# Two slots of expert 0 taken out of the routed order: found, gathered and begun inside attention

## The chip, the cores and the metric

One core of a Trainium2 chip runs the whole program in one launch. The time is device microseconds of that core; the number compared is the median over runs, and one further execution was recorded by the hardware profiler. The engines are TensorE (PE in the profile, its weight loads PEld), VectorE (DVE), ScalarE (ACT), GpSimd (POOL) and SyncE (SP, which issues most DMAs).

## The reference

Three stages follow one another. Attention runs over keys and values that are averaged over blocks of 8 positions; a mixture of 8 experts takes the best expert for each of 4,608 tokens; a dense layer of width 2,048 with a squared ReLU ends it.

```python
k_p = k.reshape(B, H, Sp, pool, D).mean(axis=3)            # 8 batches, 8 heads, 576 -> 72, D = 64
attn = softmax(scale * q @ k_p^T);  x = attn @ v_p         # x: 4608 x 512
e_idx = np.argmax(x @ w_gate, axis=1)
for e in range(E):                                         # 8 experts, 512 -> 1024 -> 512
    h = np.maximum(x[mask] @ w1[e], 0.0);  ye = h @ w2[e]
    out[mask] = gate_w[mask, None] * eom[mask, e, None] * ye
h = x @ w_in                                               # 512 -> 2048
g = s * np.maximum(h, 0) ** 2 + b;  return g @ w_out       # 2048 -> 512
```

All is in float32. Large products are taken as three products of split operands (high x high, high x low, low x high), so one product of a 128-token tile with a 512 x 1024 matrix is 24 matmuls of 128x512.

## The kernel before

**Attention** (`attention`) goes through 36 tiles of 128 tokens in one software pipeline: in turn `t` the steps `s1` to `s5` work on tiles `t+1`, `t`, `t-2`, `t-3` and `t-4`. `s5` divides by the sum of the exponentials (`rec`), writes the gate logits `lg` and the output tile `x` (L362), and SP stores `x` to DRAM (`xd`, L365). Keys and values land in four raw buffers (`krs`, `vrs`), one of them lent by the raw room of the experts' second weights. `hooks` run at the end of given turns; they load and split expert 0's first weights (`wa`).

**Routing** (`Router`) takes the tiles in six batches (8, 8, 8, 6, 4, 2 tiles). `steps` finds each token's expert (`oh`), counts with small matmuls into the PSUM tile `pr` (L565 to L579), and ranks. DVE steps of it are put singly between those of attention by `fill`. After the last batch `finish` turns ranks into slot numbers, compares them with the slot index (`ro_eq`, L676), and inverts the permutation by 40 matmuls into `inv` (L684), once for the first three slots and once for the rest; `kp_idx` (L690) is then the list of tokens of every slot, and `tables` (L717 to L740) writes which slots change expert (`kp_chg`, `kp_nxt`). Between these steps stand matmuls on the identity whose result nobody reads (`warm`, L77).

**Experts** (`experts`). The tokens of one expert fill whole slots of 128, so there are at most 43 slots; the table `total` says how many are used. For slot `i`: `gather(i)` on POOL fetches its 128 tokens (`xg`, L1009), `tr(i)` transposes them on PE (`pt`, L1018) and splits them on ACT and DVE (`xh`, `xl`, L804/L805), `l1(i)` is the first layer (24 matmuls, L1028 to L1030, into `bank`), `trh` transposes the hidden layer (`th`, L1042), `cut_h` splits it (`hh`, `hl`), and `l2` is the second layer (24 matmuls, `py`, L1058). `l2` of slot `i-1` stands between `l1(i)` and `trh` of slot `i`.

`sw1(i)` and `sw2(i)` (`switch`) are conditional: where slot `i` begins a new expert, ACT and DVE split its weights and SP loads the ones after; in any case ACT, DVE and SP read the flag `kp_chg` and branch (L855, L856). The matmuls of `l1(i)` wait for the semaphores that ACT and DVE reach behind this branch.

Into the slots `side(i, part)` puts work for later stages: a step of `Doubles` (`db.step`), which turns float64 weights of the dense stage into pairs of float32 on ACT, DVE and POOL (`dt`, `wo`; L929 to L946), and once, at slot 0, `close_ranks` (L749 to L780 on DVE), which makes the final positions and the slots' start rows.

**Order.** The program is issued as written, on five in-order engines; nothing reorders it. Buffers and waits follow from pools of tiles.

Of the kernel before, what the change touches and what calls it, by code (L numbers as in the profile page):

```python
# [49 lines left out]
def attention(ctx, tc, c, q, k, v, wg, wog, xd, lg, ro, spare, hooks):  # L50
# [21 lines left out]

    def warm(n):

        w = ps.tile([P, 512], F32, tag="pf", name="warm")
        for _ in range(n):
            nc.tensor.matmul(w[:, 0:P], lhsT=ident, rhs=ident, start=True, stop=True)  # L77
# [265 lines left out]
    def s5(t, pv):  # L343
# [16 lines left out]
        def rest():  # L360
            x = p3.tile([P, 2, 4, D], F32, tag="x", name="x", bufs=5)
# [156 lines left out]
class Router:  # L518


    def __init__(self, ctx, tc, c, lg, kp):
# [120 lines left out]
    def finish(self, psv, inv):  # L642
        nc, V, p1, kp, c = self.nc, self.nc.vector, self.p1, self.kp, self.c
# [1 line left out]
        til = p1.tile([P, E], I32, name="ro_til")
# [1 line left out]
        toff = p1.tile([P, E], F32, name="ro_toff")
        ot = p1.tile([P, E, NT], F32, name="ro_ot")
        sf = p1.tile([P, NT], F32, name="ro_sf")
# [999 lines left out]
```

## Time and profile before

| | |
|---|---|
| median of 3 runs | 1447.56 us (1447.36 to 1448.45) |
| profiled execution | 1446.02 us, span 1444.1 us |
| PE busy | 1412.4 us, 98% of the span |
| DVE, ACT, POOL busy | 828.1, 709.4, 429.3 us |
| attention and routing, to the first matmul of a slot | 0 to 200.5 us |
| experts (39 slots) | 200.5 to some 690 us |
| dense stage | to 1444 us |

The page gives the busy time of each engine, 40 slices of the span, the chain that ended last, and the costliest groups of instructions. Where PE is busy without a gap the time is the sum of its work; where it waits, the trace names the engine and line that released it. The number of slots used is the second layer's count, 624 high-half matmuls at 16 a slot: 39. The reference's own routing, with its tokens put in the order of the kernel's tiles, gives the experts 1018, 55, 333, 239, 827, 724, 24 and 1388 tokens: 8, 1, 3, 2, 7, 6, 1 and 11 slots; of the first 2,048 tokens in that order 863 go to expert 0.

### The profile page before, as it was taken

To read this page: it belongs to the slowest core of one execution; us is meant where nothing else is said; L and a number is where in the kernel's file an instruction comes from. 1 tells how busy PE (TensorE), PEld (TensorE's weight loads), DVE (VectorE), ACT (ScalarE), POOL (GpSimd) and SP (SyncE) were. 2 spreads that over 40 slices of the span, in tenths; PEclk is the share of its full clock that TensorE was granted. 3 is DMA by queue.
4 is the path that set the end of the run, shared out by engine and by line. 5 is a ranking of instruction groups with operands and counts; after the bars stand their busy time and mean duration, and the time that the engine had idled before them with its cause. 6 is when DMAs were issued, how large, how long until landed. Compare 5 with 4: busy or idle time off the path is not lost.

```text
span 1444.1 us, 23042 instructions
## 1 busy us (share of the span) xinstructions
PE 1412.4 (98%) x7612; PEld 1243.0 (86%) x7612; DVE 828.1 (57%) x1669; ACT 709.4 (49%) x1318; POOL 429.3 (30%) x579
## 2 busy tenths in 40 slices
PE   6999999999999999999999999999999999999998
PEld 5898978888888888887888988888888888889887
DVE  6788885487746567324666534634554463455333
ACT  3666623365534355223556555545555554555443
POOL 4998233444655558325320100000010000001001
PEclk9999999999999999999999999999999999999999
DMA  9995343277865768485665654465465446545441
GB/s 248 282 316 172 125 168 127 88 234 225 234 199 184 215 192 254 144 64 153 220 163 131 181 145 127 121 189 139 117 182 147 121 129 182 138 117 162 121 115 62
DMA packets 203040, 239.43 MB, mean 166 GB/s; under 512 B 66702, under 2 KB 114062, under 8 KB 202894
## 3 DMA queue, kind: packets, MB, share of 16 engines
q1 hardware_dynamic: 195502, 217.22, 54.2%
q0 software_dynamic: 7392, 20.49, 4.7%
q8 instruction: 63, 1.03, 0.3%
q14 instruction: 83, 0.68, 0.2%
HBM read 184.39 MB, written 43.83 MB: 158 GB/s over the span
## 4 chain that ended last, share of the span: by engine, by line
PE 44%; issue 8%; DVE 0%; ACT 0%; POOL 0%; DMA 0%; POOLq 0%; DVEq 0%; ACTq 0%
PE po L1439 8%; PE po L1438 8%; PE po L1437 7%; PE bank L1378 7%; PE bank L1379 7%; PE bank L1380 7%; PE py L1058 0%; POOL out L1449 0%; DMA ring<-ws 0%; DVE yo L1446 0%; POOLq L1645 0%; DVE y L1393 0%; ACT wb L1402 0%; DVE wb L1404 0%; ACT xg L1384 0%
## 5 line engine op out<-in xcount | busy, mean ns | idle before, releaser
L1401 ACT ACTIVATE r<-r,s_b 128x384 f32<-128x384 f32 x188 | 133.3, 709 | 275.4 <-DVE r L1394 247.8
L1449 POOL DMA_INDIRECT out<-yo,kp_pos x36 | 35.7, 991 | 662.9 <-ACT yo L1448 537.2
L1439 PE MATMUL po<-wo,wb 128*128 128x512 f32 x576 | 228.6, 397 | 0.0
L1438 PE MATMUL po<-wo,wb 128*128 128x512 f32 x576 | 227.6, 395 | 0.0
L1437 PE MATMUL po<-wo,wb 128*128 128x512 f32 x576 | 224.0, 389 | 0.0
L1058 PE MATMUL py<-wb,hh 128*128 128x512 f32 x624 | 191.2, 389 | 0.3 <-ACT hh L804 0.3
L1393 DVE TENSOR_TENSOR r<-bank,held 128x384 f32<-128x384 f32 x141 | 78.4, 556 | 183.1 <-PE bank L1380 181.1
L1378 PE MATMUL bank<-wa,ring 128*128 128x384 f32 x480 | 162.3, 338 | 1.0 <-ACT xg L1384 0.9
L1379 PE MATMUL bank<-wa,ring 128*128 128x384 f32 x480 | 162.1, 338 | 0.0
L1380 PE MATMUL bank<-wa,ring 128*128 128x384 f32 x480 | 161.0, 335 | 0.0
L1404 DVE TENSOR_TENSOR wb<-r,wb 128x384 fp32r<-128x384 f32 x188 | 105.3, 560 | 67.8 <-ACT wb L1402 67.4
L1058 PEld LDWEIGHTS py<-wb,hh 128*128 128x128 f32 x624 | 117.0, 188 | 24.7 <-ACT hh L804 0.5
L804 ACT ACTIVATE hh<-th 128x512 fp32r<-128x512 f32 x78 | 42.5, 595 | 180.1 <-PE th L1042 179.0
L1439 PEld LDWEIGHTS po<-wo,wb 128*128 128x128 f32 x576 | 107.9, 187 | 23.1
L1028 PE MATMUL bank<-wa,xh 128*128 128x512 f32 x312 | 125.5, 402 | 0.0
L931 POOL TENSOR_SCALAR dt<-dt 128x256 f32<-128x256 f32 x64 | 71.9, 1123 | 175.3 <-DVE dt L930 148.9
L1030 PE MATMUL bank<-wa,xl 128*128 128x512 f32 x312 | 122.1, 391 | 0.0
L1029 PE MATMUL bank<-wa,xh 128*128 128x512 f32 x312 | 121.6, 390 | 0.2 <-DVEq L856 0.2
L1058 PE MATMUL py<-wb,hl 128*128 128x512 f32 x312 | 120.5, 390 | 0.0
L1437 PEld LDWEIGHTS po<-wo,wb 128*128 128x128 f32 x576 | 108.2, 188 | 11.5
L1438 PEld LDWEIGHTS po<-wo,wb 128*128 128x128 f32 x576 | 107.9, 187 | 11.5
L1378 PEld LDWEIGHTS bank<-wa,ring 128*128 128x128 f32 x480 | 90.1, 188 | 16.2 <-ACT r L1390 4.6
(262 smaller groups left out, 2846.5 us busy)
## 6 DMA issues: line engine op xcount, KB each, us to landing
ring<-ws SPq DMA_DIRECT2D x336, 256.0 KB
wr<-in_moe_w SPq DMA_DIRECT2D x72, 512.0 KB
ws<-wf SPq DMA_DIRECT2D x16, 896.0 KB
ys<-y SPq DMA_DIRECT2D x37, 256.0 KB
xd<-x SPq DMA_DIRECT2D x36, 256.0 KB
q<-in_q SPq DMA_DIRECT2D x16, 512.0 KB
vr<-in_v SPq DMA_DIRECT2D x8, 1024.0 KB
dx<-in_moe_w_out SPq DMA_DIRECT2D x32, 256.0 KB
```

What stands on the lines that cost most here:

```text
L1028: nc.tensor.matmul(ph, lhsT=xh[:, k], rhs=wh[:, k, s], start=k == 0, stop=False)
L1029: nc.tensor.matmul(ph, lhsT=xh[:, k], rhs=wl[:, k, s], start=False, stop=False)
L1030: nc.tensor.matmul(ph, lhsT=xl[:, k], rhs=wh[:, k, s], start=False, stop=k == 3)
L1058: nc.tensor.matmul(py, lhsT=a, rhs=w, start=j == 0, stop=j == len(steps) - 1)
L1378: nc.tensor.matmul(o, lhsT=w[:, 0, k], rhs=xh[:, k], start=f, stop=False, skip_group_check=True)
L1379: nc.tensor.matmul(o, lhsT=w[:, 0, k], rhs=xl[:, k], start=False, stop=False, skip_group_check=True)
L1380: nc.tensor.matmul(o, lhsT=w[:, 1, k], rhs=xh[:, k], start=False, stop=False, skip_group_check=True)
L1401: lambda: nc.scalar.activation(out=r, in_=r, func=AF.Identity, scale=s_b[:, 0:1], bias=s_b[:, 1:2]),
L1404: [lambda: nc.vector.tensor_tensor(out=gl, in0=r, in1=gh.bitcast(F32), op=ALU.subtract)],
L1437: nc.tensor.matmul(o, lhsT=gh[:, s], rhs=wh, start=first, stop=False)
L1438: nc.tensor.matmul(o, lhsT=gh[:, s], rhs=wl, start=False, stop=False)
L1439: nc.tensor.matmul(o, lhsT=gl[:, s], rhs=wh, start=False, stop=last)
```

## The change

The first two slots are taken out of the sorted order. They hold the first 256 tokens of expert 0 among the first sixteen tiles (2,048 tokens; where there are fewer, `hole` empty places are counted to expert 0). `Router.ahead`, behind the second batch, finds them: 12 short DVE steps put between those of attention, one count and 20 inverting matmuls. `First` holds their work: two gathers on POOL at turn 28; eight transposes at turn `NT+2`, ahead of the last `s4`; the first layers of both slots (48 matmuls, `ph`), in pieces of 12, 8, 4, 8, 4 and 12 where the `warm` matmuls stood; the first slot's hidden layer transposed (`th`) and split. Expert 0's second weights are loaded and split in attention too (ACT and POOL, eight pieces each); POOL, not DVE, takes the low halves. `experts` begins with the second layer of slot 0, then the four `side` parts of slots 0 and 1, `tr(2)`, `tr(3)`, the hidden layer of slot 1, `sw1(2)`, and then the loop from slot 2.

`Router`'s tables and two buffers move into `wf`, a room kept from the start; the raw key and value buffers move into the room of the second weights; `x` has four buffers where it had five. `NSLOT` is 45 in place of 43. Line numbers of the changed kernel are its own: L541 is `First`'s first layer, L864 the inversion, L995 the low half of a split, L1058/L1059 the switch, L1228 `tr`, L1238 to L1240 `l1`, L1252 `trh`, L1268 `l2`, L1140 to L1156 `db.step`.

```diff
-    krs = [
-        one.tile([KB, NBLK, POOL * D], F32, name="kr"),
-        spare[0:KB, 0:NBLK * POOL * D].rearrange("p (j f) -> p j f", j=NBLK),
-    ]
-    vrs = [one.tile([P, NBLK, POOL * D], F32, name=f"vr{i}") for i in range(2)]
+    kv = NBLK * POOL * D
+    spare = wt.pool.tile([P, 8192], F32, tag="wb", name="kvr")
+    krs = [t[0:KB, 0:kv].rearrange("p (j f) -> p j f", j=NBLK) for t in (spare, wt.raw[1][0])]
+    vrs = [spare[:, kv * i:kv * i + kv].rearrange("p (j f) -> p j f", j=NBLK) for i in (1, 2)]
+    xbuf = [one.tile([P, DM], F32, name=f"x{i}") for i in range(3)] + [room]
+    xbuf = [t.rearrange("p (a h d) -> p a h d", a=2, h=4) for t in xbuf]
...
+        if t == 28:
+            first.gather(xd)
+        if t == NT + 2:
+            first.open()
+            first.turn(0, ps.tile([P, 512], F32, tag="pe", name="pt0"))
+            first.turn(1, ps.tile([P, 512], F32, tag="pf", name="pt1"))
...
-    warm(WARM[0])
+        if t == NT + 2:
+            first.cut(0)
     left, last = todo[:-5], todo[-5:]
     for f in last:
         f()
         if left:
             left.pop(0)()
+    first.layer(0, ps.tile([P, 2, 512], F32, tag="pv", name="ph0"))
+    first.run(12)
+    first.relu(0)
+    first.run(8)
     psv = later.pop()()
-    warm(WARM[1])
+    first.run(4)
     rest()
+    first.cut(1)
     for f in left:
         f()
+    def between():
+        first.relu(1)
+        first.layer(1, ps.tile([P, 2, 512], F32, tag="sc", name="ph1"))
+        first.run(8)
+        first.turn_h(ps.tile([P, 2, 512], F32, tag="pv", name="th0"))
+        first.run(4)
+        first.relu(0)
+    def behind():
+        first.high_h()
+        first.run(12)
+        first.relu(1)
     inv = [ps.tile([P, NSLOT], F32, tag=n, name="inv") for n in ("pq", "pe")]
-    ro.finish(psv, inv)
-    warm(WARM[2])
+    ro.finish(psv, inv, between, behind, first.low_h)
+    return first
...
+    def gather(self, xd):
+        t = self.parts(0, F32)
+        self.x = t[0:2]
+        self.hs = [t[2:4], t[0:2]]
+        for i in range(PRE):
+            self.nc.gpsimd.indirect_dma_start(
+                out=self.x[i], out_offset=None, in_=xd[0:SEEN * P, :],
+                in_offset=bass.IndirectOffsetOnAxis(ap=self.idx[:, i:i + 1], axis=0),
+            )
+    def turn(self, i, pt):
+        self.pt[i] = pt
+        for k in range(4):
+            self.nc.tensor.transpose(
+                out=pt[:, k * P:k * P + P], in_=self.x[i][:, k * P:k * P + P], identity=self.ident
+            )
+    def cut(self, i):
+        split(self.nc, *self.xs[i], self.pt.pop(i))
...
+    def layer(self, i, ph):
+        self.i, self.ph = i, ph
+        xh, xl = [x.rearrange("p (k n) -> p k n", n=P) for x in self.xs[i]]
+        wh, wl = [w.rearrange("p (k f) -> p k f", f=FE) for w in self.wt.a]
+        for n in range(2):
+            s = slice(n * 512, n * 512 + 512)
+            o = ph[:, n]
+            for k in range(4):
+                for x, w in ((xh, wh), (xh, wl), (xl, wh)):
+                    self.todo.append(
+                        lambda o=o, a=x[:, k], b=w[:, k, s], u=k == 0 and x is xh and w is wh, v=k == 3 and x is xl:
+                        self.nc.tensor.matmul(o, lhsT=a, rhs=b, start=u, stop=v)
+                    )
+    def run(self, n):
+        for _ in range(n):
+            self.todo.pop(0)()
+    def relu(self, n):
+        self.nc.scalar.activation(out=self.hs[self.i][n], in_=self.ph[:, n], func=AF.Relu)
+    def turn_h(self, th):
+        self.th = th
+        for n in range(2):
+            for k in range(4):
+                self.nc.tensor.transpose(
+                    out=th[:, n, k * P:k * P + P], in_=self.hs[0][n][:, k * P:k * P + P], identity=self.ident
+                )
+    def high_h(self):
+        for n in range(2):
+            self.nc.scalar.activation(out=self.hh[n], in_=self.th[:, n], func=AF.Copy)
+    def low_h(self):
+        for n in range(2):
+            self.nc.vector.tensor_tensor(
+                out=self.hl[n], in0=self.th[:, n], in1=self.hh[n].bitcast(F32), op=ALU.subtract
+            )
...
+PRE = 2
+SEEN = 16
+HOLE = PRE * P
+NSLOT = NT + E - 1 + PRE
+ROOM = 5120
 WIDE = 4
-SOON = 3
-WARM = (11, 12, 11)
+SOON = 5
...
+    def ahead(self, carry, alloc, later):
+        nc, V, c, kp, oh = self.nc, self.nc.vector, self.c, self.kp, self.kp["oh"]
+        hole, sf, ps = kp["hole"], self.tile([P, SEEN], F32), []
+        more = [self.tile([P, 1], F32) for _ in range(2)]
+        def settled():
+            while later:
+                later.pop()()
+            return ps[0]
+        def count():
+            ps[:] = [alloc()]
+            nc.tensor.matmul(ps[0][:, 0:E], lhsT=c["ones"], rhs=carry, start=True, stop=True)
+        def invert():
+            ps[:] = [alloc()]
+            order = [NT + t for t in range(WIDE)] + list(range(SEEN))
+            for i in order:
+                nc.tensor.matmul(
+                    ps[0][:, 0:PRE], lhsT=self.rv[:, i, :], rhs=self.eq[:, i % NT, 0:PRE],
+                    start=i == order[0], stop=i == order[-1],
+                )
+        sh = [P, SEEN, PRE]
+        return [
+            lambda: later.append(count),
+            lambda: V.tensor_scalar(
+                out=sf, in0=oh[:, 0, 0:SEEN], scalar1=-64.0, scalar2=64.0, op0=ALU.mult, op1=ALU.add
+            ),
+            lambda: V.tensor_tensor(out=sf, in0=sf, in1=self.ki[:, 0:SEEN], op=ALU.add),
+            lambda: V.tensor_scalar(
+                out=hole, in0=settled()[:, 0:1], scalar1=-1.0, scalar2=float(HOLE), op0=ALU.mult, op1=ALU.add
+            ),
+            lambda: V.tensor_tensor(
+                out=self.eq[:, 0:SEEN, 0:PRE], in0=c["iota_s"][:, 0:PRE].unsqueeze(1).to_broadcast(sh),
+                in1=sf.unsqueeze(2).to_broadcast(sh), op=ALU.is_equal,
+            ),
+            lambda: later.append(invert),
...
+            lambda: V.tensor_scalar(
+                out=kp["idx"][:, 0:PRE], in0=settled()[:, 0:PRE], scalar1=float(MID), scalar2=float(SEEN * P - 1),
+                op0=ALU.add, op1=ALU.min,
+            ),
+            lambda: V.tensor_tensor(out=more[1], in0=more[1], in1=hole, op=ALU.is_lt),
+            lambda: V.tensor_tensor(out=more[0], in0=more[0], in1=more[1], op=ALU.add),
+            lambda: V.tensor_tensor(out=self.sum[:, 0:1], in0=self.sum[:, 0:1], in1=more[0], op=ALU.add),
+            lambda: V.tensor_copy(out=carry[:, 0:1], in_=self.sum[:, 0:1]),
+        ]
...
-        compare(0, NT, 0, SOON)
+        compare(0, NT, PRE, SOON)
         for step in rows:
             step()
-        invert(inv[0], 0, SOON)
+        between()
+        invert(inv[0], PRE, SOON)
         for t in range(0, 24, 8):
             compare(t, t + 8, SOON, NSLOT)
-        index(inv[0], 0, SOON)
+        index(inv[0], PRE, SOON)
+        behind()
         compare(24, 32, SOON, NSLOT)
         compare(32, NT, SOON, NSLOT)
         invert(inv[1], SOON, NSLOT)
+        last()
         index(inv[1], SOON, NSLOT)
         self.tables()
...
+    c1 = wk[:, E + E * NT + NT:2 * E + E * NT + NT]
+    V.tensor_copy(out=c1, in_=cnt)
+    V.tensor_tensor(out=c1[:, 0:1], in0=c1[:, 0:1], in1=hole, op=ALU.subtract)
+    V.tensor_tensor_scan(out=c0, data0=c["one8"], data1=c1, initial=0.0, op0=ALU.mult, op1=ALU.add)
+    V.tensor_tensor(out=c0, in0=c0, in1=c1, op=ALU.subtract)
+    V.tensor_scalar(out=cs, in0=kp["oh"][:, 0], scalar1=hole, scalar2=None, op0=ALU.mult)
+    V.tensor_tensor(out=kp["pos"][:, SEEN:], in0=kp["pos"][:, SEEN:], in1=cs[:, SEEN:], op=ALU.subtract)
...
-    gather(0)
-    gather(1)
-    tr(0)()
     gather(2)
-    sw1(0)
-    tr(1)()
     gather(3)
-    wt.split(1)
-    sw2(0)
+    py = l2(room_y(), True, start.hh, start.hl)
+    second(1)
+    side(0, 0)
+    side(0, 1)
+    tr(2)()
+    gather(4)
+    th = trh(start.hs[1])
+    wt.raw_new(0)
+    second(0)
+    later = [tr(3)]
+    gather(5)
+    cut_h(th)
+    later.append(lambda: result(0, py))
+    side(1, 0)
+    side(1, 1)
+    sw1(2)
...
-    for i in range(NT - 1):
+    for i in range(PRE, NT - 1):
...
+        hooks.setdefault(25 + j, []).append(lambda j=j: wt.load(1, slice(0, 1), part=j))
+            hooks.setdefault(29 + j + what, []).append(lambda j=j, w=what: wt.piece(1, j, 8, w, nc.gpsimd))
```

On PE, in the routing of the last batch, the order before is this (`pr` is the last count, `tri`, `ones` and `oh` its operands, `inv` the inverted permutation):

```order
L574 MATMUL pr<-rcarry,ones 128x16
L579 LDWEIGHTS ones
L579 MATMUL pr<-oh,ones 128x8
L77 MATMUL warm<-ident 128x128 x12
L684 LDWEIGHTS rv
L684 MATMUL inv<-ro_eq,rv 128x3
```

And in the changed kernel, from the same count to the first inverting matmul (`ph_2631` and `ph_2688` are the first layers of slots 0 and 1, `th` the hidden layer of slot 0, `wf` the room that now holds the routing tables):

```order
L705 MATMUL pr<-oh,ones 128x8
L541 MATMUL ph_2631<-wa_114,first_2574 128x512 x2
L541 MATMUL ph_2631<-wa_115,first_2574 128x512
...
L541 MATMUL ph_2688<-wa_115,first_2574 128x512
L555 MATMUL th_2697<-ident,first_2066 128x128 x8
...
L541 MATMUL ph_2688<-wa_114,first_2574 128x512
L864 LDWEIGHTS wf
L864 MATMUL inv<-wf 128x3
```

Sixteen matmuls and eight transposes stand between the count and the inversion, where there were twelve `warm` matmuls.

On DVE, behind the last index, the order before has the split of slot 0's tokens (`xl`) and the switch next to the tables (`kp_nxt`, `kp_pos`); `close_ranks` (L749 and on) comes after it:

```order
L740 TENSOR_SCALAR kp_nxt<-ro_nx 1x44
L707 SCALAR_TENSOR_TENSOR kp_pos<-ki,rf 128x36
L805 TENSOR_TENSOR xl_2882<-pt,xh_2880 128x512
L855 TENSOR_LOAD kp_chg
L856 COMPARE_AND_BRANCH
```

In the changed kernel the switch that the first layer of slot 2 waits for stands behind `close_ranks` (L934 to L970, from which one row is shown), the split of slot 2's tokens and of slot 1's hidden layer (`hl`), and the four steps of `Doubles` (numbers behind a name tell buffers apart):

```order
L890 SCALAR_TENSOR_TENSOR kp_pos_92<-wf_116 128x36
...
L970 TENSOR_REDUCE kp_st_97<-dy_2919 1x1
L1140 TENSOR_SCALAR dt_2946<-dx_2841 128x256
...
L995 TENSOR_TENSOR xl0_2870<-pt_2959,xh0_2868 128x512
L995 TENSOR_TENSOR hl0_2876<-th_2967,hh0_2874 128x512
...
L1147 TENSOR_SCALAR dt_3005<-dt_3005 128x256
L1151 SCALAR_TENSOR_TENSOR dt_3005<-dx_2845,dt_3005 128x256
L995 TENSOR_TENSOR wo0_1_2840<-dt_2952,wo0_0_2839 128x256
L1058 TENSOR_LOAD kp_chg_95
L1059 COMPARE_AND_BRANCH
```

Thirty-nine DVE instructions stand between the tables and the first switch of the changed kernel, where there was one.

On PE, the changed kernel goes from the inversion straight to the second layer of slot 0 (`py`), and what follows is the first layer of slot 2, whose first matmul waits for ACT and whose second for DVE:

```order
L1268 MATMUL py_2880<-wb_2166,first01_2574 128x512 x23
L1228 MATMUL pt_2959<-ident_64,xg0_2866 128x128 [waits DMASW2_49]
L1228 MATMUL pt_2959<-ident_64,xg0_2866 128x128 x3
L1252 MATMUL th_2967<-ident_64,first00_2066 128x128 x4
L1252 MATMUL th_2972<-ident_64,first00_2066 128x128 x4
L1228 MATMUL pt_2993<-ident_64,xg1_2867 128x128 [waits DMASW3_49]
L1228 MATMUL pt_2993<-ident_64,xg1_2867 128x128 x3
L1059 UNCONDITIONAL_BRANCH
L1238 MATMUL bank0_2852<-wa0_114,xh0_2868 128x512 [waits Activation_49]
L1239 MATMUL bank0_2852<-wa1_115,xh0_2868 128x512 [waits DVE_49]
L1240 MATMUL bank0_2852<-wa0_114,xl0_2870 128x512
```

Before, the inversion was followed by `warm`, two `tr` and the first layer of slot 0.

## Rows read from the trace of the kernel before

**Rows 1.** Stretches: us, then busy us and count per engine, PEclk, DMA share.
```profile
144.00:180.00 36.00, 35.03 (x308) 33.03 (x307) 31.11 (x97) 22.33 (x60) 8.39 (x11) 1.00 0.40 127
...
187.00:201.00 14.00, 11.40 (x159) 10.39 (x157) 12.14 (x51) 0.97 (x3) 5.59 (x6) 1.00 0.43 133
```
**Rows 2.** Groups by line: busy us, mean ns, idle before.
```profile
L362 DVE TENSOR_TENSOR x<-pv,rec 128x512 f32<-128x512 f32 x36 | 24.5, 680 | 0.0
L77 PE MATMUL warm<-ident 128*128 128x128 f32 x68 | 8.3, 279 | 0.0
```
**Rows 3.** Timeline of PE, routing: start us, us, instruction, [idle before <-releaser].
```profile
186.13 0.19 PE L572 MATMUL pr<-oh,tri 128*128 128x32 bf16 x1
...
189.60 0.20 PE L569 MATMUL pr<-oh,ones 128*128 128x8 bf16 x2 [0.63 <-DVE oh L556]
...
192.77 2.31 PE L684 MATMUL inv<-ro_eq,rv 128*128 128x3 f16 x80
...
198.84 0.63 PE L1018 MATMUL pt<-ident,xg 128*128 128x128 f32 x4 [1.21 <-DVE ro_le L734]
...
200.51 0.47 PE L1028 MATMUL bank<-wa,xh 128*128 128x512 f32 x1
201.21 0.50 PE L1029 MATMUL bank<-wa,xh 128*128 128x512 f32 x1 [0.23 <-DVEq L856]
```
**Rows 4.** Timeline of PE, second layer of slot 0 to first layer of slot 2.
```profile
214.31 0.62 PE L1058 MATMUL py<-wb,hh 128*128 128x512 f32 x2
...
219.76 1.03 PE L1042 MATMUL th<-ident,hs 128*128 128x128 f32 x8
220.63 0.60 PE L1018 MATMUL pt<-ident,xg 128*128 128x128 f32 x4
220.98 0.48 PE L1028 MATMUL bank<-wa,xh 128*128 128x512 f32 x1
```
**Rows 5.** Timeline of DVE, from the last ranks to the first steps of Doubles.
```profile
186.46 0.19 DVE L619 TENSOR_TENSOR rmine<-pr,oh 128x32 f32<-128x32 f32 x1 [0.61 <-PE pr L579]
...
190.12 0.17 DVE L652 TENSOR_SCALAR ro_til<-pr 128x8 int32<-128x8 f32 x1
...
194.00 0.15 DVE L690 TENSOR_SCALAR kp_idx<-inv 128x3 int32<-128x3 f32 x1
...
195.12 0.20 DVE L690 TENSOR_SCALAR kp_idx<-inv 128x40 int32<-128x40 f32 x1 [0.34 <-issue]
...
199.03 0.18 DVE L707 SCALAR_TENSOR_TENSOR kp_pos<-ki,rf 128x36 int32<-128x36 int32 x1
200.24 0.69 DVE L805 TENSOR_TENSOR xl<-pt,xh 128x512 fp32r<-128x512 f32 x1 [1.03 <-ACT xh L804]
...
207.98 0.17 DVE L749 TENSOR_TENSOR_SCAN dy<-one,kp_cnt 128x8 f32<-128x8 f32 x1
...
213.17 0.27 DVE L930 TENSOR_SCALAR dt<-dx 128x256 int32<-128x256 int32 x1
213.37 1.27 DVE L805 TENSOR_TENSOR hl<-th,hh 128x512 fp32r<-128x512 f32 x2
```
**Rows 6.** Timeline of POOL, a gather and one step of Doubles.
```profile
195.06 1.20 POOL L1009 DMA_INDIRECT xg<-xd,kp_idx  x1 [1.91 <-DMA dx<-in_moe_w_out]
...
216.00 1.08 POOL L931 TENSOR_SCALAR dt<-dt 128x256 f32<-128x256 f32 x1
217.04 0.85 POOL L946 TENSOR_TENSOR dt<-dt,dx 128x256 int32<-128x256 int32 x1
```
**Rows 7.** A stretch near the start, as rows 1.
```profile
31.20:34.60 3.40, 3.40 (x15) 3.17 (x14) 2.89 (x9) 0.58 (x1) 0.00 (x0) 0.50 1.08 226
```
**Rows 8.** Timeline of PE around that stretch.
```profile
30.73 0.28 PE L168 MATMUL prl<-ident,kp 72*128 72x72 f32 x1 [1.92 <-ACT kbd L163]
...
31.37 2.13 PE L278 MATMUL sc<-kbd,qT 128*128 128x144 f32 x8
...
36.79 1.15 PE L278 MATMUL sc<-kbd,qT 128*128 128x144 f32 x8
```

More of the change, by code (lines that the diff above doesn't have):

```diff
@@ L71, in attention @@
     vps = [one.tile([P, NBLK + 1, D], F32, name=f"vp{i}") for i in range(2)]
[L73 to L77, printed above, removed]
     def load_kv(b, src, dst, n, j0=0, j1=NBLK):
@@ L360, in rest @@
         def rest():
[L361 removed]
+            x = xbuf[t % 4]
             nc.vector.tensor_tensor(
@@ L426, in attention @@
     later = []
+    first = First(nc, ident, wt, ro.kp["idx"])
     for t in range(NT + 4):
@@ new lines, in behind, with __init__, parts, open @@
+    def behind():
+        first.high_h()
+        first.run(12)
+        first.relu(1)
+    inv = [ps.tile([P, NSLOT], F32, tag=n, name="inv") for n in ("pq", "pe")]
+    ro.finish(psv, inv, between, behind, first.low_h)
+    return first
+class First:
+    def __init__(self, nc, ident, wt, idx):
+        self.nc, self.ident, self.wt, self.idx = nc, ident, wt, idx
+        self.pt, self.todo = {}, []
+    def parts(self, i, dt):
+        t = self.wt.raw_tile(0, i, dt, "first")
+        return [t[:, DM * j:DM * j + DM] for j in range(4)]
+    def open(self):
+        t = self.parts(1, F32R)
+        self.xs = [t[0:2], t[2:4]]
+        self.hh, self.hl = self.xs
+    def gather(self, xd):
[48 more added lines that the diff above has]
+            )
@@ L609, in steps @@
                 out += self.row(t)
-        return out
+        if b == SEEN:
+            out += self.ahead(carry, alloc, later)
+        return out
+    def ahead(self, carry, alloc, later):
[32 more added lines that the diff above has]
+            lambda: later.append(invert),
+            lambda: V.tensor_scalar(out=hole, in0=hole, scalar1=0.0, scalar2=None, op0=ALU.max),
+            lambda: V.tensor_tensor(out=more[0], in0=c["pvec"], in1=hole, op=ALU.is_lt),
+            lambda: V.tensor_scalar(out=more[1], in0=c["pvec"], scalar1=float(P), scalar2=None, op0=ALU.add),
+            lambda: V.tensor_scalar(
[7 more added lines that the diff above has]
+        ]
@@ L640, in row, with finish @@
         ]
[L642 to L643 removed]
+    def finish(self, psv, inv, between, behind, last):
+        nc, V, kp, c, eq = self.nc, self.nc.vector, self.kp, self.c, self.eq
         a, b = BATCHES[-1]
[L645 removed]
+        til = self.tile([P, E], I32)
         self.tend = kp["tend"]
[L647 to L650 removed]
+        toff = self.tile([P, E], F32)
+        ot = self.tile([P, E, NT], F32)
+        sf = self.tile([P, NT], F32)
         offsets = [
@@ L848, in split, with switch @@
             s = slice(j * 4096 // n, (j + 1) * 4096 // n)
-            split(self.nc, w[0][:, s], w[1][:, s], self.raw[i][:, s], eng)
-    def switch(self, i, chg, nxt, first):
+            split(self.nc, w[0][:, s], w[1][:, s], self.part_of(i, s), eng)
+    def switch(self, i, chg, nxt):
         nc = self.nc
@@ L857, in switch @@
             e = nc.values_load(nxt, engines=[ENG.SP], min_val=0, max_val=E - 1)
-            if first:
-                self.load(i, bass.ds(e, 1))
             for j in range(4):
                 self.split(i, j, j + 1)
-                if not first:
-                    self.load(i, bass.ds(e, 1), part=j)
+                self.load(i, bass.ds(e, 1), part=j)
 CW = 256
@@ L903, in more, with rest @@
         self.wo += [[w[:, r] for w in t] for r in range(n)]
+    def rest(self, ctx):
+        n = 2 * (FF // P - len(self.wo))
+        t = self.room.tile([P, 2048 + 28 * P], F32R, tag="wf", name="wo_wf")
+        t = [t[:, DM * i:DM * i + DM] for i in range(11)]
+        pool = ctx.enter_context(self.tc.tile_pool(name="wo_rest", bufs=1))
+        t += [pool.tile([P, DM], F32R, name=f"wo_{i}") for i in range(11, n)]
+        self.wo += [t[i:i + 2] for i in range(0, n, 2)]
     def load(self, n):
@@ L1619, in tail @@
             db.run(db.end, len(db.pieces))
-        experts(x, tc, c, kp, wt, xd, ys, bank, wide, side, ahead, tail)
+        experts(x, tc, c, kp, wt, xd, ys, bank, wide, side, ahead, tail, start)
     dn.run(ctx)
```

151 lines of the change are left out of this document (87 added, 64 removed).

## The prediction, made before the changed kernel ran

> **What bounds the kernel now.** I read the busy time by stage first, then PE's timeline through the routing, then DVE's and POOL's. In attention's second half PE is busy 35.0 of 36 us while DVE has 31.1, ACT 22.3 and POOL 8.4 [rows 1]: PE sets the pace. In the routing, 187 to 201 us, PE shows 11.4 of 14 us, but that is padding: the 34 `warm` matmuls are 68 records and 8.3 us [rows 1, 2]. The chain there is DVE's: last ranks at 186.46, totals at 190.12, indices at 194.00 and 195.12, tables done at 199.03 [rows 5]. A gather issued at 195.06 is transposed at 198.84, and the first layer of slot 0 starts at 200.51 [rows 3, 6]. From there PE is full: a layer of 24 matmuls takes 214.31 to 219.76, 5.45 us or 0.227 each, and the first layer of slot 2 starts at 220.98 [rows 4]. All work behind that point is the same in both kernels (39 slots, the first expert change at slot 8), so the change is worth what it does to 220.98.
>
> One more row decides much. The second matmul of slot 0's first layer (L1029) needs only `xh` and weights, yet it started at 201.21 after a wait for "DVEq L856" [rows 3]: 0.28 us after the end of `xl` (200.24 + 0.69) [rows 5], which is the DVE instruction ahead of the switch. A first layer waits until DVE has gone through its switch, whether or not weights change.
>
> **The change part by part.** I follow the chain in the clock of the profiled execution, 1446.0 us with a span of 1444.1; the median of the runs stands 1.5 us above that, and the shift found here is added to the median.
>
> *Attention.* `ahead` gives PE 20 inverting matmuls at 2.31/80 us [rows 3], 0.6 us, on the bound. Its 12 DVE steps of some 0.2 us (like L652, 0.17 [rows 5]) fall between dependent steps of attention; DVE has 4.9 us free in 36 [rows 1]. I take 0; were none hidden, 2.4. The eight copies on ACT and eight subtractions on POOL lie in 13.7 and 27.6 free us of 36 [rows 1]; I take 0. With four `x` buffers for five, `x` may wait for a store; before it never did (0.0 idle [rows 2]). No row prices it. A whole tile's `x`, 0.68 us [rows 2], at a few of the early tiles where DMA is fullest (share 1.08 [rows 7]) would be 2; the row nearest is the 0.0, and I take 0.3 for both unknowns together. So attention ends 0.6 later, and 0.3 goes to the end of the sum.
>
> *First layers in the routing.* Eight transposes take 0.87 us (219.76 to 220.63 [rows 4]) ahead of the last `s4`, so the count at 186.13 [rows 3] moves to 187.6. Then 20 matmuls of slot 0, the third of which waits for a low half on DVE: 0.6 us, as an `xl` takes 0.69 [rows 5] and two matmuls run meanwhile. 187.6 + 0.15 + 20 x 0.227 + 0.6 = 192.9 for the last count, which was at 189.60 [rows 3]. DVE's own chain is ready a little earlier, so PE sets this. Up to the inversion stand 16 matmuls and eight transposes: 3.6 + 0.9 + 0.1 = 4.6 us, to 197.5, against 192.77 [rows 3]; DVE needs only 2.65 us for its part (190.12 to 192.77 [rows 3, 5]). The first index follows 1.23 us later (192.77 to 194.00 [rows 3, 5]): 198.8. The gather and its landing take 194.00 to 198.84 [rows 3, 5], so slot 2's tokens are there at 203.6, in time. PE does half of the 80 inverting matmuls (1.1 us), 12 of slot 1 (2.7), the other half (1.1): 202.4. The second index moves from 195.12 [rows 5] to 202.6.
>
> *What PE then has.* Second layer of slot 0, 5.45; two groups of four transposes at 0.35 (220.63 to 220.98) and eight at 0.87 [rows 4]: free at 209.4. If nothing held it, slot 2 would begin 11.6 us earlier than at 220.98.
>
> *What DVE has first.* Behind the second index: the tables, 195.12 to 199.03 and one step, 4.0 us, 0.1 more for 45 slots: 206.7. `close_ranks`, 207.98 to 213.17 or 5.2 us [rows 5], which before lay beside PE's first layer of slot 1; with five more steps of 0.2 it is 6.3: 213.0. Then the four steps of `Doubles`, tied to POOL: 0.3 for the first `dt` on DVE and 0.2 for POOL to start; two L931 at 1.04 (216.00 to 217.04), one L946 at 0.85, two gathers at 1.2 and the space behind each, 2.5, one L931 and one L946 again, 1.9 [rows 6]; an ACT copy and the last `wo` on DVE, 0.4 each (half of the 0.69 of a 128x512 step [rows 5], and a little), and the switch 0.3. Sum 9.0. DVE's own work there (`xl` 0.6, the two `hl` 1.27 [rows 5], ten short steps) fits beside. The switch is passed at 222.0, where the like matmul before stood at 220.98 + 0.23 = 221.2. So slot 2 begins 0.8 us later than before, and PE waits for 12.6 us (209.4 to 222.0): all that the routing hides is given back behind it. In place of `warm`, PE stands still in front of `close_ranks`.
>
> *The clock.* In 31.2 to 34.6 us the granted clock was 0.50, the 1.2 GHz level [rows 7]; just before it PE had waited 1.92 us [rows 8]. Eight L278 took 2.13 us in it and 1.15 outside [rows 8]: 0.46 of the time at that level is lost. A stretch as long as that row's, 3.4 us, costs 1.6 us, two cost 3.1, and none 0; the wait here is six times the 1.92, so I take a little more than one, 2.1. The Trainium skill, page "TensorE: Matmul & The Clock Gate", section "HAM oscillation — how this bites in real kernels", says that an idle gap re-throttles the array and that the cost of coming back is paid after each. The trace agrees (0.50 behind a wait); by that rule the sum is as here, and without it 2.1 less.
>
> *Sum:* 0.8 + 0.3 + 2.1 = +3.2 us. In the profile's terms 1449.2, as a median 1450.8. Its own range: the unhidden bounds (+2.4, +1.7, +1.0) are unlikely together, and the chain of some thirty short durations may be off by 2 either way, the clock by 2.1 downwards: 1447 to 1454.
>
> **Rivals.**
>
> *The switch does not hold the first layer.* Then slot 2 starts when its own `xl` is split: DVE 213.0 + 2.4 (first `dt` to the second step's last row, with POOL's L931 between) + 0.7 = 216.1, third matmul, so 215.6 for the first: 5.4 us earlier, less 0.3 and 2.1 (PE still waits 6 us): 1444.6; with the clock kept, 1442.5. It decides from the point where PE's wait on DVE is met ahead of L1058. Against it is the 0.23 us at L1029 [rows 3]; for it, that one short wait is all the evidence. Chance 0.13.
>
> *The hiding works as drawn.* PE goes on at 209.4: 1447.6 - 11.6 + 0.3 = 1436.3. It needs DVE and POOL to take less than half of what their rows say. Chance 0.04.
>
> *Attention slows.* Each of the three engines beside PE gets work there; with the two upper bounds, 2.4 and 1.7, and a little of ACT's copies, another 4 us: 1454.8. For it: DVE is at 86% [rows 1] and `x` is its largest single step. Against: no gap on PE there before. Chance 0.14.
>
> *The slots don't fill.* Were fewer than 256 tokens of expert 0 in the first sixteen tiles, a slot more would be computed, 2 x 5.45 + 0.87 + 0.35 = 12.1 us [rows 4]: 1463. The reference's routing has 863 of them. Chance 0.01.
>
> **How the numbers follow.** A measurement of this kernel tells 0.2%, 2.9 us, from no change. The main case has 0.68: with +3.2 and 2 us of doubt about 0.37 of it all is slower, 0.30 the same, 0.01 faster. The first rival is split, 0.08 faster and 0.05 the same; the second is faster, 0.04; the third slower, 0.12, and 0.02 the same; the fourth slower. Together 0.13 faster, 0.37 the same, 0.50 slower. The range 1444.0 to 1455.0 leaves out the second rival, the first with the clock kept, and the ends of the third.
>
> **What would show it.** Right: the second index near 202.6; PE idle for some 12 us or more with L1238 or L1239 released by the switch (DVEq or ACTq L1059); the clock at 0.50 right behind; the first layer of slot 2 near 222. `close_ranks` must stand on DVE while PE waits. Wrong: PE going from `tr(3)` into L1238 with no gap; a DVE row of L357 with idle time, or PE gaps between 100 and 180 us; an inversion later than 198, by which PE's matmuls would hold the chain longer than I take; 40 slots in the second layer's count.

## The result and the profile after

The changed kernel takes 1455.61 us (median of six runs, 1453.35 to 1458.03), the kernel before on the same chip 1447.92 (1447.07 to 1449.03): a ratio of 1.0052, 95% interval 1.0039 to 1.0065, or +7.7 us. Forecast were +3.2, slower as the likeliest side, with a range that ended 0.6 below the median. The execution that was profiled is the quickest of the six, 1453.35, with a span of 1451.5; its mean granted clock is 0.994, as in one other, and 0.991 in the four slower ones.

The same stretches of attention and routing as in [rows 1], then PE's wait in front of slot 2, and two stretches at the 1.2 GHz level (us, then busy us and count for PE, PEld, DVE, ACT and POOL, the granted clock, DMA share, GB/s):

```profile
144.00:180.00 36.00, 33.06 (x283) 31.15 (x282) 30.24 (x86) 23.28 (x59) 13.59 (x15) 0.95 0.31 103
187.00:201.00 14.00, 11.82 (x72) 8.95 (x71) 12.01 (x45) 2.45 (x5) 4.87 (x6) 1.00 0.34 116
215.40:227.10 11.70, 0.20 (x2) 0.00 (x0) 8.54 (x27) 2.02 (x6) 7.58 (x8) 0.70 1.02 363
220.05:230.25 10.20, 3.08 (x7) 2.27 (x8) 5.45 (x13) 1.16 (x3) 7.21 (x8) 0.50 0.97 354
165.45:168.80 3.35, 3.35 (x15) 3.08 (x14) 1.26 (x5) 0.00 (x0) 0.00 (x0) 0.50 0.24 83
```

Two things are to be seen. The wait in front of slot 2 (third line) is there as forecast. But in attention, where PE had 35.03 us of 36 [rows 1], it now has 33.06, and the clock fell there too. PE's timeline from the routing on, to be held against [rows 3, 4]:

```profile
197.94 0.20 PE L695 MATMUL pr<-oh,ones 128*128 128x8 bf16 x2
...
202.70 1.16 PE L864 MATMUL inv<-wf 128*128 128x3 f16 x40
...
208.12 5.73 PE L1268 MATMUL py<-wb,first 128*128 128x512 f32 x24 [0.41 <-DVE kp_idx L870]
...
215.00 0.60 PE L1228 MATMUL pt<-ident,xg 128*128 128x128 f32 x4
227.17 0.80 PE L1238 MATMUL bank<-wa,xh 128*128 128x512 f32 x1 [11.57 <-ACTq L1059]
```

The first layer of slot 2 starts at 227.17 instead of 220.98 [rows 4]. From the second index on, the chain is the forecast one: index 207.78, ranks closed 218.29, last step 226.97 (DVE's rows), so 19.4 us from the index to slot 2, and 202.6 to 222.0 was forecast. What is late is the index itself, by 5.2 us. The cause stands in one DVE row of attention and one of the routing. DVE, then POOL at the same time:

```profile
160.44 2.71 DVE L1044 TENSOR_TENSOR wa<-wr,wa 128x512 fp32r<-128x512 f32 x1
163.08 0.15 DVE L341 TENSOR_SCALAR rec<-pv 128x8 f32<-128x8 f32 x1
163.26 0.20 DVE L343 RECIPROCAL rec<-rec 128x8 f32<-128x8 f32 x1
163.50 0.29 DVE L346 TENSOR_TENSOR lp<-pv,rec 128x128 f32<-128x128 f32 x1
...
186.89 3.03 DVE L671 TENSOR_TENSOR wf<-lg,wf 128x32 f32<-128x32 f32 x1
189.84 0.28 DVE L346 TENSOR_TENSOR lp<-pv,rec 128x128 f32<-128x128 f32 x1
```

```profile
160.11 2.49 POOL L1044 TENSOR_TENSOR wb<-wr,wb 128x512 fp32r<-128x512 f32 x2
163.20 1.27 POOL L1044 TENSOR_TENSOR wb<-wr,wb 128x512 fp32r<-128x512 f32 x1 [0.60 <-ACT wb L1042]
...
186.15 3.73 POOL L1044 TENSOR_TENSOR wb<-wr,wb 128x512 fp32r<-128x512 f32 x3
```

L1044 on DVE has a median of 0.684 us over its eight instructions and here takes 2.71; L671 on 32 columns takes 0.18 in experiment 4 and here 3.03. Both end with POOL's row of subtractions, or about one own length after it. Both have two operands in SBUF. L343, with one such operand, and L346, with one in PSUM, take their usual time beside POOL's subtraction of 163.20. PE then waited for 2.06 us, and behind this wait its granted clock was 0.50 for 3.4 us (the last line of the stretches above):

```profile
161.74 1.15 PE L273 MATMUL sc<-kbd,qT 128*128 128x144 f32 x8
164.94 1.39 PE L329 MATMUL pv<-vbd,eT 128*128 128x162 f32 x5 [2.06 <-DVE vbd L208]
```

A wait of this kind is booked as busy time of the waiting instruction. It isn't found under idle time or releasers, only by a duration that departs from that of its like.

How far attention has come in each trace is read from the start of DVE's multiplication that writes `x` (L362 before, L357 after), tile by tile:

```
tile    before   after    after - before
27      158.30   157.89   -0.41
28      162.49   164.12   +1.63
30      170.79   174.09   +3.30
33      181.99   185.29   +3.30
34      184.43   190.55   +6.12
35      189.47   195.43   +5.96
```

From tile 27 to 30 it loses 3.7 us (2.71 - 0.68 of waiting and half of 3.35 us at half clock), from 33 to 34 another 2.8 (3.03 - 0.18): 6.5 us together. (At tile 7 this execution led by 2.27, from the first 50 us, where the kernel before twice ran for 3.4 us at 0.50 and this execution did not; at tile 27 it has 0.41 of it left. Some 0.6 of what was lost between is the price of the 20 added matmuls, as experiment 4 shows; for the rest no cause was found.)

### The profile page after: what moved, and what is told of

Same layout as the page of the kernel before. It is cut to its first block, busy times and chain, and to the rows that moved or that the text cites. A ratio compares the mean times of both kernels' runs of the same rounds, so it can differ in the third digit from the quotient of the medians.

```text
span 1451.5 us, 22908 instructions
## 1 busy us (share of the span) xinstructions
PE 1405.8 (97%) x7565; PEld 1235.3 (85%) x7565; DVE 829.8 (57%) x1680; ACT 710.3 (49%) x1324; POOL 438.5 (30%) x587
## 4 chain that ended last, share of the span: by engine, by line
PE 43%; issue 8%; ACT 1%; POOL 0%; DVE 0%; DMA 0%; POOLq 0%; DVEq 0%; ACTq 0%
PE po L1651 8%; PE po L1650 8%; PE po L1649 7%; PE bank L1590 7%; PE bank L1591 7%; PE bank L1592 7%; PE py L1268 0%; POOL out L1661 0%; DMA ring<-ws 0%; ACT wb L1614 0%; ACT y L1613 0%; ACT r L1613 0%; POOLq L1856 0%; ACT yo L1660 0%; ACT hs L1613 0%
## 5 line engine op out<-in xcount | busy, mean ns | idle before, releaser
L1268 PE MATMUL py<-wb,hh 128*128 128x512 f32 x608 | 186.3, 389 | 0.3 <-ACT hh L994 0.3
L1650 PE MATMUL po<-wo,wb 128*128 128x512 f32 x396 | 156.5, 395 | 0.0
L1651 PE MATMUL po<-wo,wb 128*128 128x512 f32 x360 | 143.0, 397 | 0.0
L1649 PE MATMUL po<-wo,wb 128*128 128x512 f32 x360 | 140.0, 389 | 0.0
L1268 PEld LDWEIGHTS py<-wb,hh 128*128 128x128 f32 x608 | 114.0, 188 | 24.1 <-ACT hh L994 0.5
L1238 PE MATMUL bank<-wa,xh 128*128 128x512 f32 x296 | 119.7, 404 | 11.6 <-ACTq L1059 11.6
L1268 PE MATMUL py<-wb,hl 128*128 128x512 f32 x304 | 117.4, 390 | 0.0
L1240 PE MATMUL bank<-wa,xl 128*128 128x512 f32 x296 | 116.3, 393 | 0.0
L1239 PE MATMUL bank<-wa,xh 128*128 128x512 f32 x296 | 115.9, 391 | 0.0
L1590 PEld LDWEIGHTS bank<-wa,ring 128*128 128x128 f32 x480 | 90.1, 188 | 16.0 <-ACT r L1602 4.7
L1614 ACT ACTIVATE wb<-r 128x384 fp32r<-128x384 f32 x188 | 98.9, 526 | 6.0
L1591 PEld LDWEIGHTS bank<-wa,ring 128*128 128x128 f32 x480 | 90.1, 188 | 10.4
L995 DVE TENSOR_TENSOR hl<-th,hh 128x512 fp32r<-128x512 f32 x76 | 48.9, 683 | 82.6 <-ACT hh L994 82.6
```

The source lines that it names most:

```text
L1238: nc.tensor.matmul(ph, lhsT=xh[:, k], rhs=wh[:, k, s], start=k == 0, stop=False)
L1239: nc.tensor.matmul(ph, lhsT=xh[:, k], rhs=wl[:, k, s], start=False, stop=False)
L1240: nc.tensor.matmul(ph, lhsT=xl[:, k], rhs=wh[:, k, s], start=False, stop=k == 3)
L1268: nc.tensor.matmul(py, lhsT=a, rhs=w, start=j == 0, stop=j == len(steps) - 1)
L1590: nc.tensor.matmul(o, lhsT=w[:, 0, k], rhs=xh[:, k], start=f, stop=False, skip_group_check=True)
L1591: nc.tensor.matmul(o, lhsT=w[:, 0, k], rhs=xl[:, k], start=False, stop=False, skip_group_check=True)
```

## The experiments

Two theories of the lateness stood against each other. P: POOL's subtraction keeps a DVE instruction waiting that has two operands in SBUF (where the kernel's tiles lie). W: attention and routing are late by the added work. On the wait in front of slot 2, S says that it is DVE's queue ahead of the switch, R that something else holds slot 2 or that time won there comes back later. All ratios are to the kernel before on the same chip, with the 95% interval.

**1. The low halves on DVE.**

```diff
-hooks.setdefault(29 + j + what, []).append(lambda j=j, w=what: wt.piece(1, j, 8, w, nc.gpsimd))
+hooks.setdefault(29 + j + what, []).append(lambda j=j, w=what: wt.piece(1, j, 8, w))
```

> The eight subtractions that make the low halves of expert 0's second weights in attention go back from POOL to DVE (0.68 us each there, 5.4 in all). Theory P (POOL's subtraction keeps a DVE instruction with two SBUF operands waiting until POOL is through its row of them): the 2.71 us L1044 near 160 us and the 3.03 us L671 near 187 us are 0.68 and 0.2 again, PE's wait of 2.06 at 164.9 and the 0.50 clock behind it are gone; DVE's 5.4 us more give 1 to 3 back; median 1450 to 1453. Theory W (attention and the routing are late by the added work itself: 20 matmuls, DVE's and ACT's added steps): DVE has more to do still, 1456 to 1460.

1453.01 us, 1.0033 (1.002 to 1.0046). DVE's longest L1044 is 0.93, the L671 of the last batch but one 0.18, and PE's gaps from 150 us to the second layer of slot 0 are under 0.8. The rows are those of P. By the ratios it is 2.7 us less than the changed kernel, although DVE has 5.4 us more to do; the two intervals overlap, but none of the five executions (1449.64 to 1453.41) reaches the 1456 of W.

**2. The same subtractions on POOL, apart from DVE's.**

```diff
-hooks.setdefault(20 + 2 * j + what, ...wt.piece(0, j, 8, w))
+hooks.setdefault(18 + 7 * j // 5 + what, ...wt.piece(0, j, 8, w))
-hooks.setdefault(29 + j + what, ...wt.piece(1, j, 8, w, nc.gpsimd))
+hooks.setdefault(29 + 2 * j // 3, ...wt.piece(1, j, 8, w, nc.gpsimd))
```

> POOL keeps the eight subtractions; the eight pieces of the first weights are split earlier (hooks 18 to 28 instead of 20 to 35) and the second weights' pieces come at three in two tiles (hooks 29 to 33 instead of 29 to 37), so that hardly any DVE instruction with two SBUF operands stands beside a POOL subtraction. The same work in both. Theory P: attention ends some 3 us earlier and the last batch's chain another 2.5, 1449 to 1452. Theory W: 1455 to 1457, as after the change.

1450.11 us, 1.0026 (1.0014 to 1.0038). The two long rows are gone (longest left: L1044 1.13, L682 0.94). Attention falls back 2.1 us between tiles 15 and 27, 0.6 of it as in experiment 4; the rest goes with the earlier pieces, three of which now meet POOL's averaging of keys and take 0.93, 0.94 and 1.13 us. With the same work, the order of two engines' rows alone gave back half: here the intervals don't overlap, and W falls.

**3. POOL's subtractions twice.**

```diff
 hooks.setdefault(29 + j + what, ...wt.piece(1, j, 8, w, nc.gpsimd))
+if what:
+    hooks[30 + j].append(lambda j=j: wt.piece(1, j, 8, 1, nc.gpsimd))
```

> Each of POOL's eight subtractions is issued twice. Theory P: the DVE instruction that meets them waits for twice as many in a row: 2.5 us more near 160 us and up to 3.8 more near 187 us, 1459 to 1464. Theory W: POOL has free time for 8 x 1.27 us there, 1455 to 1457.

1455.64 us, 1.0063 (1.005 to 1.0076): the number of W, and not that of P. P missed the size here, and the trace tells how. DVE in this kernel:

```profile
160.83 1.45 DVE L1044 TENSOR_TENSOR wa<-wr,wa 128x512 fp32r<-128x512 f32 x1
...
185.09 0.55 DVE L671 TENSOR_TENSOR wf<-lg,wf 128x32 f32<-128x32 f32 x1
185.57 0.28 DVE L346 TENSOR_TENSOR lp<-pv,rec 128x128 f32<-128x128 f32 x1
185.77 1.22 DVE L675 TENSOR_TENSOR wf<-wf,desc 128x32 f32<-128x32 f32 x1
```

```profile
160.47 11.08 POOL L1044 TENSOR_TENSOR wb<-wr,wb 128x512 fp32r<-128x512 f32 x8
```

DVE still waits, but now gets in behind the first subtraction: 0.77 us near 160 instead of 2.03, and more, shorter waits near 186. What counts is how many of POOL's instructions a DVE instruction has to sit out, not how many there are.

**4. POOL writes the same tiles and reads nothing.**

```diff
+if eng is not None:
+    eng.memset(w[1][:, s].bitcast(F32), 0.0)
+    return
 (eng or self.nc.vector).tensor_tensor(out=w[1][:, s], ...
```

> POOL's eight subtractions become eight memsets of the same tiles: POOL writes as much and reads nothing of SBUF. The low halves of expert 0's second weights are zero by it, so that part of the sum is left out for expert 0. Theory P in the Trainium skill's form (a DVE instruction with two SBUF inputs waits for a POOL instruction that reads SBUF, not for one that only writes): no L1044 over 0.7 and no L671 over 0.3 us, no gap on PE at 162 to 165, 3 to 5 us less than the changed kernel: 1450 to 1453. If any POOL instruction on those tiles did it, or POOL's time alone: waits stay, 1455 to 1457.

1449.15 us, 1.0008 (0.9999 to 1.0017), so 6.5 us less than the changed kernel (some 4 to 9 with both intervals). POOL and DVE:

```profile
160.49 2.37 POOL L1045 MEMSET wb<- 128x512 f32 x5
...
182.85 1.44 POOL L1045 MEMSET wb<- 128x512 f32 x3
```

```profile
160.87 0.68 DVE L1047 TENSOR_TENSOR wa<-wr,wa 128x512 fp32r<-128x512 f32 x1
...
183.62 0.18 DVE L671 TENSOR_TENSOR wf<-lg,wf 128x32 f32<-128x32 f32 x1
```

POOL writes while DVE reads two operands, and DVE doesn't wait: it is not the writing that held it, and not the tiles. The wait hangs on the operands that POOL's subtraction reads.

The traces show less than 6.5 us: slot 2 starts 4.9 us earlier (222.32 against 227.17). That the table above also comes to 6.5 is chance, for part of DVE's wait near 187 was no loss. In experiment 4 attention falls back by 1.4 us between tiles 34 and 35, where DVE waits 1.48 us for PE (at L800, 187.36), which has the eight transposes to do first; in the changed kernel PE did them while DVE stood at L671.

The Trainium skill, page "SBUF — State Buffer", section "Who interferes with whom", states that a DVE instruction with two SBUF inputs contends with a GpSimd instruction that reads SBUF, not with one that only writes. The traces agree for the subtractions and for the writes. They don't agree with "until the first finishes" (same page, section "Summary: rules for kernel authors"): in 2.71 and 3.03 us DVE sat out two and three subtractions of 1.27 us. Nor does every POOL instruction that reads SBUF hold DVE. L816, which reads one such tensor (`iota_r`, with a value per partition beside it), takes 0.8 us on POOL; in the changed kernel DVE instructions with two operands pass beside it in their usual time. POOL, then DVE:

```profile
194.08 1.61 POOL L816 TENSOR_SCALAR wf<-iota_r,wf,num 128x128 f16<-128x128 bf16 x2 [4.21 <-DVE wf L807]
```

```profile
194.72 0.17 DVE L671 TENSOR_TENSOR wf<-lg,wf 128x16 f32<-128x16 f32 x1
194.93 0.17 DVE L675 TENSOR_TENSOR wf<-wf,desc 128x16 f32<-128x16 f32 x1
...
195.34 0.18 DVE L682 TENSOR_TENSOR oh<-wf 128x16 bf16<-128x16 f32 x1
```

Shown to hold DVE is thus POOL's subtraction, which reads two tensors. No experiment put an instruction that reads one in its place.

**5. A write between POOL's subtractions.**

```diff
 (eng or self.nc.vector).tensor_tensor(out=w[1][:, s], ...
+if eng is not None:
+    eng.memset(self.nil, 0.0)          # 128x8, a scratch tile
```

> Behind each of POOL's eight subtractions POOL writes zeros to 8 columns of a scratch tile (an instruction that reads nothing). Theory G (DVE waited through two and three subtractions because they stood back to back, each beginning before the one ahead had ended; with an instruction between them that reads nothing DVE gets in after one): L1044 near 160 us 1.5 to 2.0 instead of 2.71, L671 near 187 us 0.7 to 1.4 instead of 3.03, PE's gap near 164 under 1.2 us: 2 to 4 us less than the changed kernel, 1451.5 to 1453.5. If POOL keeps the port over such a gap as well: waits as before, 1455 to 1457.

1452.43 us, 1.0035 (1.0022 to 1.0049): the time of theory G (its interval overlaps the changed kernel's), but only half of its rows.

```profile
160.10 2.73 DVE L1045 TENSOR_TENSOR wa<-wr,wa 128x512 fp32r<-128x512 f32 x1
...
186.55 0.57 DVE L672 TENSOR_TENSOR wf<-lg,wf 128x32 f32<-128x32 f32 x1
187.05 0.28 DVE L346 TENSOR_TENSOR lp<-pv,rec 128x128 f32<-128x128 f32 x1
187.25 1.15 DVE L676 TENSOR_TENSOR wf<-wf,desc 128x32 f32<-128x32 f32 x1
```

Near 160 DVE still sits out two subtractions (PE's gap stays 2.08 us); near 186 it gets in after one. When it is let in stays open.

**6. The switch first.**

```diff
 second(1)
-side(0, 0)
-side(0, 1)
 tr(2)()
 ...
 cut_h(th)
+sw1(2)
+side(0, 0)
 later.append(lambda: result(0, py))
-side(1, 0)
-side(1, 1)
-sw1(2)
+put_off = {2: (0, 1), 3: (1, 0), 4: (1, 1)}     # one more step behind slots 2, 3 and 4
```

> The switch of the first weights for slot 2, and what its first layer needs, stand ahead of the closing of ranks and of the first step of the doubles; three further steps are put behind slots 2, 3 and 4. Theory S (the 11.6 us that PE waits in front of slot 2 is DVE's queue ahead of the switch, and nothing else holds it): tables end at 211.9, low halves to 217.2, the first layer of slot 2 starts at 217 to 218.5 instead of 227.2, PE waits 2 to 3 us; 9 to 11 us off, 1444 to 1447. Rival R (the deferred steps on DVE and POOL come back as waits in the slots behind, or a transfer of weights holds slot 2): 1451 to 1456.

1442.80 us, 0.9967 (0.9954 to 0.998). PE's timeline:

```profile
211.30 5.73 PE L1268 MATMUL py<-wb,first 128*128 128x512 f32 x24 [0.40 <-DVE kp_idx L870]
...
218.18 0.60 PE L1228 MATMUL pt<-ident,xg 128*128 128x128 f32 x4
219.23 0.49 PE L1238 MATMUL bank<-wa,xh 128*128 128x512 f32 x1 [0.45 <-ACTq L1059]
220.24 0.50 PE L1239 MATMUL bank<-wa,xh 128*128 128x512 f32 x1 [0.52 <-DVEq L1059]
```

From the second index to slot 2 it takes 8.3 us (210.96 to 219.23), in the changed kernel 19.4 (207.78 to 227.17). That is 11.1 of the 12 us by which the ratios differ. Another 0.7 come from slot 2's first layer, 6.4 us instead of 7.1: the granted clock is 1.00 in it and in front of it. (POOL's subtractions stand where they stood: L671 takes 3.05 us here too, and from 194.5 us on the granted clock was 0.50 for 3.4 us.) The deferred steps cost nothing that shows: S holds, R falls.

**7. Only the ranks behind the switch.**

```diff
 def side(i, part):
-    if i == 0: close_ranks(tc, c, wide(), kp)      # called behind sw1(2) instead
     db.step()
```

> Of the changed kernel only the closing of ranks (6.4 us on DVE) moves behind the switch for slot 2; the four steps of the doubles stay ahead of it. Theory S: the switch comes 6.4 us earlier, at 220.8, PE waits 5 us instead of 11.6 and the clock's stretch behind it is shorter; the first relu of slot 2 on DVE is due at 227, when the ranks are just closed: 6 to 8 us less than the changed kernel, 1448 to 1450. Rival: the steps' chain through POOL, not DVE's own work, holds the switch: at most 2 us less, 1453.5 to 1456.

1448.21 us, 1.0012 (1.0003 to 1.0021), 5.8 less than the changed kernel.

```profile
215.54 0.60 PE L1228 MATMUL pt<-ident,xg 128*128 128x128 f32 x4
221.29 0.80 PE L1238 MATMUL bank<-wa,xh 128*128 128x512 f32 x1 [5.15 <-ACTq L1059]
```

From the second index (208.35) to slot 2: 12.9 us, 6.5 less than 19.4, where the closing of ranks takes 6.4. Steps and ranks add up on DVE; neither hides the other.

**8. PE kept busy in its wait.**

```diff
+for _ in range(45):
+    nc.tensor.matmul(bank[0][:, 0:P], lhsT=ident, rhs=ident, start=True, stop=True)
 side(1, 0)
```

> 45 dummy matmuls of 128 columns on PE (11 us) fill its wait in front of the first layer of slot 2; nothing else moves. The granted clock behind it stays at 1.00 and the first layer of slot 2 takes 5.5 us instead of 7: 1.5 us less than the changed kernel, 1453.5 to 1455. If the clock there is worth what the prediction took, 2.1 less, 1453.5; if the matmuls hold something up, as much as or more than the changed kernel, 1455.5 to 1457.

1453.31 us, 1.0038 (1.0024 to 1.0051): about 2 us less than the changed kernel, but the intervals overlap, so the gain isn't clear of noise. The execution that was profiled is the slowest of the seven, 1459.57. In it PE was busy for 11.24 of 12 us at 1.00, 1.51 us of the wait were left over, and the clock fell all the same, for one stretch of 3.4 us inside slot 2's first layer:

```profile
220.00:232.00 12.00, 11.24 (x101) 11.05 (x99) 8.81 (x29) 2.65 (x7) 6.89 (x8) 1.00 0.98 344
234.65:238.00 3.35, 3.35 (x9) 2.64 (x8) 0.00 (x0) 0.53 (x2) 0.00 (x0) 0.50 0.40 152
```

That layer took 7.6 us (232.75 to 240.37), where 5.5 was expected and the changed kernel has 7.1. So the time is the expected one, but the row is not. The other six executions have a mean granted clock of 0.996 to 0.997 (this one 0.995), and no trace of them was kept: what the clock costs here is not settled by this run.

**9 to 11. The two cures together.** Experiments 2 and 6, 1 and 6, 5 and 6 in one kernel each.

> The edit that keeps POOL's subtractions apart from DVE's and the one that puts the switch first, together. If their causes are independent their gains add: before the change 1447.6; the first alone stood 3.7 us nearer to it than the changed kernel, the second 4.8 below it: 1438 to 1441. If they overlap (what one saves the other had hidden): 1442 to 1444.

> The low halves on DVE and the switch first, together. Added up: 1439 to 1442, some 1 us behind the kernel that keeps the subtractions on POOL but apart, since DVE pays 5.4 us for them. Overlapping causes: 1443 to 1445.

> The switch first, and the writes between POOL's subtractions, together: what the second is worth beside the changed kernel comes off the 1442.8 of the first alone: by theory G 1439 to 1441, level with the kernel that keeps the subtractions apart (1438.2); otherwise 1442 to 1444.

1438.15 us (0.9939, 0.9922 to 0.9956), 1439.26 (0.9941, 0.9927 to 0.9955) and 1440.37 (0.9949, 0.9935 to 0.9962). The gains add, within the intervals (added up, the ratios give 0.9941, 0.9948 and 0.9950): the two causes are independent. All three are quicker than both kernels; among them the intervals don't decide. In the first, slot 2 starts at 212.26, 8.7 us ahead of [rows 4]; of the 11.3 us of the rival "hiding works as drawn" 8.8 are reached once the order on DVE lets it.

## Why the prediction was wrong

It was right on the side, the wait and its cause, and wrong in one term. The time missed by 4.5 us (7.7 instead of 3.2); the term missed by 6.5, and the rest of the sum came out lower than forecast, 1.2 instead of 3.2.

- **The step that failed** is in the part on attention: "The eight copies on ACT and eight subtractions on POOL lie in 13.7 and 27.6 free us of 36 [rows 1]; I take 0." POOL had that time, and DVE paid for it: 6.5 us by the runs of experiment 4, 4.9 in the traces. The term was priced by the free time of the engine that got the work. The question that was not asked is what DVE does at that time, and whether the trace of before has two such instructions beside each other. It has, three times between 115 and 135 us, and there POOL paid. DVE of the kernel before, and POOL, at one of the three:

```profile
125.17 0.68 DVE L841 TENSOR_TENSOR wa<-wr,wa 128x512 fp32r<-128x512 f32 x1
```

```profile
124.50 0.73 POOL L133 TENSOR_TENSOR wr<-wr 126x256 f32<-126x256 f32 x1
125.30 0.86 POOL L134 TENSOR_TENSOR wr<-wr 126x128 f32<-126x128 f32 x1
...
127.46 0.46 POOL L134 TENSOR_TENSOR wr<-wr 126x128 f32<-126x128 f32 x1
```

L134 takes 0.455 us (median) and here 0.86, beside L841. The exclusion was in the trace, with POOL as the one that waits, and from 154 us to the gathers at 195 POOL had only L635 to do, which did not slow an L841 beside it (0.69 at 177.65). A maximum that is nearly twice the median was the row to read; the term's bound should have been a few of POOL's subtractions.
- **Everything else in the sum.** With the reads taken away (experiment 4) the chain can be held against the forecast point by point: counts at 187.03 (187.6 forecast) and 193.44 (192.9), the inversion at 198.21 (197.5), the second index at 203.31 (202.6), PE free at 210.9 (209.4), ranks closed at 213.83 (213.0), slot 2 at 222.32 (222.0). By the runs it stands 1.2 us above the kernel before (-0.1 to 2.5); forecast were 3.2, outside that interval. The traces give more: slot 2 starts 1.3 us later than before (222.32 against 220.98) and its first layer takes 8.0 us instead of 5.6, 3.7 together. But the profiled execution of the kernel before, 1446.02, lies 1.9 below the median on experiment 4's chip, so single executions compared can be off by as much.
- **Attention's 0.6** for the 20 matmuls: between tiles 7 and 27 experiment 4 falls back by 0.63 us against the kernel before, and the 20 matmuls take 0.65 in its trace.
- **`close_ranks` 6.3, the steps 9.0, PE's wait 12.6:** measured 6.4 (211.86 to 218.29), 9.1 (218.29 to 227.38) and 11.57.
- **The clock, 2.1:** the granted clock was 0.50 from 220.0 to 230.2, most of it in the wait. The 24 matmuls of slot 2's first layer took 7.1 us instead of the 5.6 that they took before (220.98 to 226.56): 1.5. In the traces of experiments 7 and 4 they took 7.5 and 8.0, so 1.9 and 2.4. The sign and the size hold.
- **"Attention slows"** came nearest, 1454.8, but that is luck, for its mechanism is another: experiment 4 has the same copies, DVE steps and `x` rooms, and falls back by no more than 0.03 us between tiles 27 and 34. What the prediction holds against it, "no gap on PE there before", is misread: PE of the kernel before has gaps of 0.87, 0.39 and 0.61 us near 119, 124 and 128 us and of 0.66 near 176. So gaps between 100 and 180 us were no sign by themselves; the one of 2.06 was. **"The switch does not hold the first layer"** is refuted by experiments 6 and 7.

## What to carry to other kernels

Before work moves to an idle POOL, look at what DVE does at the same time: if both read two operands from SBUF, as the subtractions here do, DVE's waits for one or several of POOL's, and a short DVE instruction on the path pays POOL's long time. Set the two apart in the order (experiment 2), or let POOL do what only writes (experiment 4). And where a change frees one engine early, list what the engine that must release it still has queued: here 15.5 us on DVE gave back all that the routing had hidden, and one reordering won it.

## What was not expected of the hardware

A DVE instruction of 0.18 us was held for 2.85 us by three subtractions on POOL in a row (3.03 in all), while in other kernels the like got in after one (0.55, 0.57). Each subtraction takes POOL 1.27 us and DVE 0.68. In experiment 3, where every second one writes the tile of the one ahead, DVE got in early; with an unrelated write between them, only at one of two places. What decides it was not found.
